# A chunk-selecting attention with a gated convolution: convolution tiles of 64 by 32, score blocks of one bank pair, stores issued by ScalarE

## The chip, the cores and the metric

The kernel runs on one core of a Trainium2 chip. A core has five engines with an instruction stream each: TensorE (PE, with weight loads shown apart as PEld), VectorE (DVE), ScalarE (ACT), GpSimd (POOL) and SyncE (SP, which here only issues transfers). Sixteen DMA engines move the data. TensorE writes to PSUM, eight banks of 128 partitions by 512 fp32 columns, and the other engines empty them. The metric is the device time of one execution in microseconds; less is better.

## The reference, cut to what matters

Attention over 4 batches of 8 heads, 768 positions of 64 values. Each query takes the six chunks of 32 keys with the highest bound on their scores. The output of all heads, 512 channels, then passes a causal convolution of five taps for each channel, a sigmoid gate and two products with 512 by 512 weights.

```python
ub = sum(maximum(q * k_min, q * k_max))          # for each query and chunk of 32 keys
top_chunks = argsort(where(causal, ub, -1e9))[..., -6:]
mask = sel(top_chunks) & (pos[:, None] >= pos[None, :])
attn = softmax(where(mask, scale * q @ k.T, -1e9))
x = (attn @ v).transpose(0, 2, 1, 3).reshape(B, S, H * D)
for k in range(5):
    gate_pre += conv_w[k] * xp[:, k:k + S, :]     # xp: x with four zero rows ahead
out = (sigmoid(gate_pre) * (x @ w_val)) @ w_out
```

## The kernel before, in words

The work is cut into 16 pairs of heads (`p`), four for each batch. The two heads of a pair lie in the two halves of the 128 partitions (`HP`). For a pair: keys and queries are loaded and transposed on PE (`tr`, line 534), copied out by ACT (540, 576) and reduced by chunk on DVE (546); POOL makes the operands of the chunk bounds (`ksmall`); PE forms the bounds (652 and 667), DVE takes the best eight and compares with the sixth (`cmp`, 716) into `NS`; PE transposes `NS` (726) and the copy is the mask `MT`. `score` writes transposed scores into PSUM: queries against keys (748), then the mask times the table `E` (757) into the same bank. ACT takes the exponential (766), POOL clears the upper triangle of the diagonal blocks (774), PE multiplies with the values (`av`, 797), DVE normalizes (806). The result `on` is brought to channels by time, `xT`, by a transposing DMA (827), for the last pair by PE (822).

`BANKS` lays the lower triangle of scores out in six banks for each head. In the kernel before, `DUO` takes two banks at a time: the score products use tiles of 64 rows by 128 columns, two at once, and the mask products use tiles of 32 by 128, four at once, one for each head and bank. For that `cmp` writes the comparison twice, 32 columns apart.

The convolution multiplies shifted copies of `xT` with diagonal matrices. The letter of `CONV` says how, pair by pair:

- Q (pairs 0 to 10, and 15), `convq`, line 883: tiles of 64 by 64, four at once. The weights are split into a high and a low half-precision part, so ten terms. `swap` (849) makes a copy of `xT` with its partition halves exchanged, `XQ`.
- S (pairs 11 to 14), `conv`, line 863: tiles of 128 by 32, four at once, six steps. Its operand `XS` holds 32 channels in four versions (two time shifts, two for high and low weights). It is made by a detour: `xw` (839) writes `xT` to a scratch tensor in DRAM, `xs` (845) reads it back in four transfers.

The diagonal matrices are built on POOL early in the kernel: `WQ` (476) in ten products, `WD` (445) in four. ACT then takes the tanh (889). For each batch, PE forms the values (`val`, 913), DVE gates them (921), PE multiplies with the output weights (937), ACT copies out with a factor of 0.5 (947; in the last batch DVE every second one, 944), and SP stores (952), 24 stores in all.

The order of each engine's stream is computed when the kernel is built. `graph` lists operations with an engine, an estimated length and a sort key from `PERIOD`, `OFF` and `DELTA`; `Graph.schedule` runs a small model of the engines, the banks and the DMA queue, and starts on each free engine the ready operation with the lowest key. Each engine then executes its stream strictly in that order. All the transfers but the two weight loads (`w_big`, on POOL) stand in SP's stream.

Of the kernel before, what the change touches and what calls it, by code (L numbers as in the profile page):

```python
# [19 lines left out]
CH = 32  # L20
# [13 lines left out]
XN = S + 6  # L34

# [15 lines left out]

DUO = ((0, 1), (2, 3), (4, 5))
SCORE = [0.68, 0.70, 0.54]
# [3 lines left out]
for _bi, _segs in enumerate(BANKS):  # L57
    for _col, _jt, _q0, _n in _segs:
        for _i in range(_n // 128):
# [5 lines left out]
PERIOD = 12.9223  # L65
OFF = dict(wdg=199.168, wbig=-116.538, cw=-683.48, load=-91.162, ktr=-51.291, qtr=99.521, kev=-172.346,
           qev=175.061, ksm=-204.505, spl=464.719, vc=678.633, ub=-186.285, top=322.7, selT=-163.727,
           sc=-181.883, ex=-292.07, av=82.464, nrm=333.712, tox=-546.25, xs=-141.243, conv=13.848,
           tanh=-338.872, val=266.063, gv=171.155, out=288.504, ev=-184.148)
# [11 lines left out]
CONV = "QQQQQQQQQQQSSSSQ"  # L81

DELTA = dict(
    wdg=(-1.243, -0.346, -5.29, 3.059, -8.51, 0.295, -11.031, 1.615, 2.466, -0.239, -5.796, 0, -2.239, 11.59,
        -0.038, 0),
    wbig=(0, 0.188, -10.953, -0.19, 0.733, -1.414, -3.353, 1.285, -5.523, -4.485, 38.175, 5.823, 4.557,
        -13.478, 0.421, 0),
    cw=(-18.314, -8.891, -8.843, -0.026, -0.2, 7.762, 12.344, 5.613, 0.06, -2.242, -4.873, -3.047, -3.366,
        0.828, -9.749, -0.011),
    load=(0.214, -1.353, 0.394, -9.477, -20.991, -15.326, -0.566, -8.721, 0.066, -10.887, 23.08, 13.879, 6.207,  # L90
        -4.098, -7.797, -2.716),
    ktr=(3.721, -2.57, -4.059, 0.646, -13.55, 0, 0.055, -1.62, -0.373, 0.436, -1.532, 6.05, 2.065, 1.379, 2.36,
        0.267),
    qtr=(-5.316, -3.862, 0.606, 2.517, 0.494, 0.207, -0.25, -17.411, 1.198, 7.239, -4.482, 0.617, -1.715,
        -0.705, 1.938, 2.43),
    kev=(0, -2.085, -0.198, 0.772, 0.854, 1.732, -0.381, -2.561, 0.048, 6.873, -0.748, -3.931, -1.54, -5.598,
        0, 0),
    qev=(-0.006, -7.153, 2.8, -8.078, -1.913, -4.426, -6.52, -0.93, -1.584, 0.557, 6.224, 0.433, 0, 0.167,
        0.325, 1.843),
    ksm=(-0.516, 1.719, 1.719, 0, -8.166, 5.024, -7.553, -5.823, 0, -13.821, -3.788, 0, 0, 0, 6.169, -3.771),  # L100
    spl=(0, 0, 0.913, -1.823, 3.174, 0.698, 2.737, 0, -0.344, -1.736, -3.55, 8.03, 12.699, 0.056, 12.489, 1.296),
    vc=(-5.408, 8.102, -1.641, -3.236, -11.492, -2.331, -9.437, 2.42, -16.561, 6.032, 0, -2.029, 9.507, 2.124,
        11.374, 1.314),
    ub=(0, 5.87, -1.717, -6.846, -10.954, -7.75, -4.319, 18.215, 2.367, -3.332, -1.487, -3.834, 2.838, -3.08,
        -3.376, 6.316),
    top=(0.011, -14.157, -0.748, -6.694, 0, 1.128, -0.085, 25.804, -19.326, 6.323, 7.216, 7.115, 6.031, 0,
        17.873, -1.714),
    selT=(0.159, 4.322, -11.032, -3.664, 2.206, 2.91, 4.105, -0.067, 0, 2.718, -8.959, -6.512, 0.16, 8.002,
        -0.12, -1.732),
    sc=(2.402, 2.062, 3.966, 0.001, -31.282, -1.168, -3.404, 9.113, -1.06, 0.639, 4.728, -3.231, -1.122,  # L110
        -0.658, -0.515, 0.885),
    ex=(-2.337, 0.461, 5.963, 6.189, 0.222, 2.13, 5.144, 9.503, 6.939, 0.624, 0.959, -13.542, -6.471, -4.563,
        6.731, -4.322),
    av=(0.086, -0.585, 2.526, 2.997, -2.315, -1.993, -1.22, 0, 3.593, 0, 0.163, -0.487, -7.862, -6.595, 1.978,
        -0.201),
    nrm=(-6.208, 0.692, -9.254, 2.271, -0.558, 4.28, 2.998, -3.761, 1.41, 1.599, -8.131, 15.962, -6.789,
        -7.511, -3.999, -3.399),
    tox=(-0.124, 4.074, 0.356, 0.146, 0, -8.203, -3.783, -8.724, -14.631, -6.792, 4.598, -8.206, -0.922,
        -1.434, -0.461, 1.278),
    xs=(-2.03, -2.537, 6.003, -3.321, -6.852, 156.074, 8.152, -17.228, -0.596, 0.102, -1.967, -1.865, -3.351,  # L120
        -1.967, -6.798, 4.494),
    conv=(-1.279, -0.745, -0.991, 1.197, -2.443, 4.986, 5.472, 4.646, -0.942, 1.84, 7.166, -0.096, 2.503,
        -1.052, 4.405, 6.594),
    tanh=(2.324, 0.747, -0.277, -2.803, 0, -3.819, -9.599, -8.531, -3.417, -0.893, -3.327, -0.726, -11.212,
        -0.762, 0.19, -5.493),
    val=(9.122, 0, -6.241, -3.696, 12.326, 2.893, 6.691, -2.508, -1.856, -2.108, -6.259, 37.115, 3.96, 9.385,
        10.567, 13.154),
    gv=(0.221, -7.002, -6.129, -3.775, -3.838, 1.864, 0, 7.518, 5.786, 5.443, -1.952, 0.455, 3.175, 0.33,
        -10.961, 5.879),
    out=(1.189, 1.43, -6.802, 3.456, 1.001, 0.92, -7.795, 60.654, -9.234, 0.84, 0.994, -0.377, 1.598, -2.455,  # L130
        -0.186, 1.785),
    ev=(-3.564, -1.25, -5.306, -0.157, 0, -6.542, 10.476, 4.737, 0.526, 6.5, 7.77, 0.056, 0, 0.402, 3.529,
        -0.709),
)
# [185 lines left out]
def graph(off, period, nbuf):  # L320
# [649 lines left out]
    for o in later:  # L970
        o.deps.add(byname["ksm1"])
# [170 lines left out]
```

## Time and profile before

| | |
|---|---|
| three runs, us | 195.68, 196.44, 196.68 (median 196.44) |
| the profiled execution, us | 197.75 |
| its span, first to last instruction, us | 196.0 |
| TensorE clock granted | 1.0 throughout |
| moved by DMA | 36.01 MB, mean 184 GB/s |
| read from and written to HBM | 24.16 MB and 7.08 MB |

The times are of whole executions; the trace covers the span of the one profiled. Busy time is counted for each engine apart, and a busy TensorE is not one at its peak, since matmuls are pipelined. A group of instructions is given with its line, engine, operation, tiles and number, then its total busy time in us and the mean length of one in ns, then the idle time of the engine ahead of it and what ended that. The chain is followed back from the last instruction, at each step to what released it.

### The profile page before, as it was taken

How to read it: one execution, taken by the hardware profiler on the slowest of the kernel's cores; microseconds unless marked ns; L12 is line 12 of the kernel's file. 1: busy time of each engine (PE TensorE's matmuls, PEld its weight loads, DVE VectorE, ACT ScalarE, POOL GpSimd, SP SyncE). 2: the span in 40 equal slices, each digit the busy share in tenths (PEclk: the TensorE clock that was granted, in tenths of full speed). 3: DMA queues.
4: the chain of work that ended last, by engine and by line, in shares of the span. 5: the costliest groups of instructions: out<-in, count | busy, mean ns of one | idle time of the engine just before them, and what ended most of it. 6: DMA issues, size and time to landing. Idle time of an engine off the chain costs nothing.

```text
span 196.0 us, 7461 instructions
## 1 busy us (share of the span) xinstructions
PE 184.8 (94%) x2926; PEld 118.4 (60%) x2926; DVE 148.3 (76%) x476; ACT 146.7 (75%) x326; POOL 90.4 (46%) x189
## 2 busy tenths in 40 slices
PE   7989898979999999999999999999999997899992
PEld 3666666656757675686675677577656462555540
DVE  6897588979999988879998558998899614062451
ACT  4458999989778879895969897677988977633421
POOL 5589999888445344547262137414363212100000
PEclk9999999999999999999999999999999999999999
DMA  5999999989989998969796998230218839777225
GB/s 134 269 269 207 163 211 205 255 161 225 236 147 222 151 279 190 262 142 222 198 257 181 251 221 162 58 70 2 47 48 251 117 92 282 221 261 251 106 110 211
DMA packets 94917, 36.01 MB, mean 184 GB/s; under 512 B 88226, under 2 KB 91298, under 8 KB 94882
## 3 DMA queue, kind: packets, MB, share of 16 engines
q1 hardware_dynamic: 93826, 34.48, 74.5%
q0 software_dynamic: 1056, 1.05, 3.8%
q8 instruction: 23, 0.38, 0.8%
q14 instruction: 12, 0.10, 0.2%
HBM read 24.16 MB, written 7.08 MB: 159 GB/s over the span
## 4 chain that ended last, share of the span: by engine, by line
PE 74%; DVE 12%; DMA 5%; ACT 4%; SPq 2%; issue 2%; DVEq 0%
PE b L883 10%; PE b L913 10%; PE b L937 9%; PE b L797 9%; PE b L748 8%; PE b L534 8%; PE b L757 5%; PE b L652 5%; DMA xT<-on 3%; DVE km L546 3%; ACT P L766 2%; DMA XS<-scr 2%; PE b L726 2%; PE b L1011 2%; PE b L352 2%; DVE NS L716 2%
## 5 line engine op out<-in xcount | busy, mean ns | idle before, releaser
L766 ACT ACTIVATE P<-b 128x512 f16<-128x512 f32 (+1 forms) x192 | 88.9, 570 | 9.8 <-PE b L757 4.7
L774 POOL TENSOR_SCALAR_AFFINE_SELECT P<-P 128x512 f16<-128x512 f16 (+1 forms) x64 | 33.8, 550 | 60.5 <-ACT P L766 60.4
L546 DVE TENSOR_REDUCE km<-b 128x12 f32<-128x384 f32 x64 | 31.9, 548 | 6.7 <-PE b L534 2.8
L748 PE MATMUL b<-Qh,Kh 64*128 64x128 f16 (+3 forms) x384 | 28.8, 258 | 0.9 <-ACT P L766 0.4
L797 PE MATMUL b<-VA,P 128*128 128x65 f16 x672 | 28.0, 194 | 0.5 <-ACT P L766 0.4
L797 PEld LDWEIGHTS <-P 128*128 128x128 f16 x672 | 24.8, 98 | 4.1 <-issue 1.8
L921 DVE SCALAR_TENSOR_TENSOR gv<-g,b 128x384 f16<-128x384 f32 x32 | 17.5, 550 | 10.2 <-PE b L913 9.1
L913 PE MATMUL b<-xT,wval 128*128 128x384 f16 x128 | 23.8, 326 | 0.0
L937 PE MATMUL b<-wout,gv 128*128 128x512 f16 x96 | 23.5, 379 | 0.0
L947 ACT ACTIVATE osb<-b 128x512 f32<-128x512 f32 x21 | 12.8, 623 | 13.8 <-PE b L937 11.7
L889 ACT ACTIVATE g<-b 128x384 f32<-128x384 f32 x32 | 14.4, 495 | 10.2 <-PE b L883 7.6
L883 PE MATMUL b<-xT,WQ 64*64 64x384 f16 x240 | 21.8, 325 | 0.0
L883 PE MATMUL b<-XQ,WQ 64*64 64x384 f16 x240 | 21.8, 325 | 0.0
L540 ACT ACTIVATE Kh<-b 128x384 f16<-128x384 f32 x32 | 16.2, 520 | 7.0 <-PE b L534 5.2
L748 PEld LDWEIGHTS <-Kh 64*128 64x128 f16 x384 | 12.0, 94 | 12.8 <-issue 11.3
L806 DVE TENSOR_TENSOR on<-b,rcp 128x384 f16<-128x384 f32 x32 | 17.8, 557 | 1.1
L576 ACT ACTIVATE Qh<-b 128x384 f16<-128x384 f32 x32 | 15.7, 531 | 2.7 <-PE b L534 2.7
L757 PE MATMUL b<-MT,E 32*128 32x128 f16 (+4 forms) x352 | 17.6, 259 | 0.0
L883 PEld LDWEIGHTS <-WQ 64*64 64x64 f16 x480 | 12.8, 106 | 6.8 <-issue 2.0
L913 PEld LDWEIGHTS <-wval 128*128 128x128 f16 x128 | 11.5, 98 | 7.9 <-issue 1.3
L622 DVE SCALAR_TENSOR_TENSOR rl<-Qh,ql 128x640 f16<-128x640 f16 x16 | 15.9, 994 | 0.2
L534 PE MATMUL b<-ident,kn 128*128 128x128 f32 x96 | 15.1, 282 | 0.1
(102 smaller groups left out, 320.8 us busy)
## 6 DMA issues: line engine op xcount, KB each, us to landing
kn<-in_k_dram SPq DMA_DIRECT2D x32, 192.0 KB, 3.7
qn<-in_q_dram SPq DMA_DIRECT2D x32, 192.0 KB, 3.7
vn<-in_v_dram SPq DMA_DIRECT2D x16, 384.0 KB, 5.1
out_dram<-osb SPq DMA_DIRECT2D x24, 256.0 KB, 3.1
XS<-scr SPq DMA_DIRECT2D x16, 193.3 KB, 3.3
XQ<-xT SPq DMA_DIRECT2D x24, 96.8 KB, 2.5
scr<-xT SPq DMA_DIRECT2D x4, 193.5 KB
wval<-in_moe_w_val_dram POOLq DMA_DIRECT2D x1, 512.0 KB, 8.6
```

The source lines that it names most:

```text
L534: t.nc.tensor.matmul(out=b[:, j * 128:(j + 1) * 128], lhsT=vv(name, p)[:, 3 * w + j, :], rhs=t.ident, is_transpose=True, start=(j == 0), s ...
L546: t.nc.vector.tensor_reduce(out=vv("km", p)[:, i, w * 12:(w + 1) * 12], in_=bank(("kn", p, w))[:, 0:HB].rearrange("p (c t) -> p c t", t=CH ...
L748: t.nc.tensor.matmul(out=bank(("s", p, bi, hh))[:, col:col + n], lhsT=kh[HP[hh], jt * 128:(jt + 1) * 128], rhs=qh[HP[hh], q0:q0 + n], star ...
L757: t.nc.tensor.matmul(out=bank(("s", p, bi, hh))[:, col + m0 - q0:col + n], lhsT=t.E[rows, jt * 128:(jt + 1) * 128], rhs=mt[rows, m0 - 128: ...
L766: t.nc.scalar.activation(out=t.P[p % 2][hh][bi], in_=bank(("s", p, bi, hh))[:, 0:n], func=AF.Exp, scale=0.125 / QS)
L774: t.nc.gpsimd.affine_select(out=ap, in_=ap, pattern=[[0, n], [1, 128]], compare_op=ALU.is_ge, fill=0.0, base=0, channel_multiplier=-1)
L797: t.nc.tensor.matmul(out=b[:, qt, :], lhsT=t.P[p % 2][hh][bi][:, col:col + 128], rhs=vv("VA", p)[:, hh, jt, :], start=(jt == 0), stop=(jt ...
L806: t.nc.vector.tensor_tensor(out=vv("on", p)[:, :, hh * 64:(hh + 1) * 64], in0=b[:, :, 0:D], in1=rc.unsqueeze(2).to_broadcast([128, NT, D]) ...
L883: t.nc.tensor.matmul(out=bank(("cv", p, r))[HP[c], 0:HB], lhsT=t.WQ[HP[r], k // KSZ, k % KSZ, (p % 4) * 2 + c, :], rhs=x[HP[r], a:a + HB], ...
L913: t.nc.tensor.matmul(out=k[:, 0:HB], lhsT=t.wval[:, ct, et * 128:(et + 1) * 128], rhs=t.xT[:, (4 * b_ + ct) % 8, XL + w * HB:XL + (w + 1) ...
L921: t.nc.vector.scalar_tensor_tensor(out=vv("gv", 4 * b_ + et)[:, sl], in0=vv("g", 4 * b_ + et)[:, sl], scalar=1.0, in1=bank(("val", b_, et, ...
L937: t.nc.tensor.matmul(out=k, lhsT=vv("gv", 4 * b_ + et)[:, s * 128:(s + 1) * 128], rhs=t.wout[:, et, :], start=(et == 0), stop=(et == NCT - 1))
```

## The change

The change replaces four things and computes the order anew.

1. `CONV` becomes R for pairs 0 to 14 and stays Q for pair 15. R uses tiles of 64 rows by 32 columns. The 64 rows are 32 channels twice, for the high and the low part of the weights; the two halves of the partitions hold the two halves of time. Five taps, four groups of channels and two halves of time make 40 matmuls. The diagonal matrices are five products of 128 by 512 on POOL; for the Q of the last pair there are two of 128 by 640.
2. The detour writes `xT` as it lies, 128 partitions outermost, and reads back four transfers of 32 partitions by four runs of 388 elements.
3. `score` takes one bank of each head at a time, and both its products use tiles of 64 by 128. `cmp` writes once.
4. The output stores are issued by ACT, except every second one of the last batch, which stays on SP. The two weight loads become two operations that wait for later pairs.

`PERIOD`, `OFF`, `DELTA` and some of the estimated lengths have new values.

```diff
-DUO = ((0, 1), (2, 3), (4, 5))
-SCORE = [0.68, 0.70, 0.54]
+SCORE = [0.40, 0.435, 0.442, 0.445, 0.35, 0.325]
-CONV = "QQQQQQQQQQQSSSSQ"
+CONV = "RRRRRRRRRRRRRRRQ"
...
-        for j in range(4):
-            G.op(f"wdiag{j}", "POOL", 0.8, 12.3 + 0.1 * j, w_diag(j), r=[("wsel",)], w=[("WD",)])
+        for j in range(KSZ):
+            later.append(G.op(f"wdiag{j}", "POOL", 1.0, key("wdg", 2, 0.5 * j), w_diag(j), r=[("wsel",)], w=[("WD",)]))
...
         for m in range(2):
-            for k in range(KSZ):
-                later.append(G.op(f"qdiag{m}{k}", "POOL", 1.0, key("wdg", 2, 0.5 * (m * KSZ + k)), q_diag(m, k), r=[("qw",)],
-                                  w=[("WQ",)]))
+            last.append(G.op(f"qdiag{m}", "POOL", 1.3, key("wdg", 6, m), q_diag(m), r=[("qw",)], w=[("WQ",)]))
...
-            for r in range(2):
-                t.nc.vector.tensor_tensor(
-                    out=vv("NS", p).rearrange("p i (s c) -> p i s c", s=2)[:, :, :, CH * r:CH * r + NCH],
-                    in0=src,
-                    in1=vv("top", p)[:, :, :, 5:6].to_broadcast([128, NIT, 2, NCH]), op=ALU.is_lt)
+            t.nc.vector.tensor_tensor(
+                out=vv("NS", p).rearrange("p i (s c) -> p i s c", s=2)[:, :, :, 0:NCH],
+                in0=src,
+                in1=vv("top", p)[:, :, :, 5:6].to_broadcast([128, NIT, 2, NCH]), op=ALU.is_lt)
...
+        def score(bi, p=p):
+            def emit():
+                nc, kh, qh, mt = t.nc, vv("Kh", p), vv("Qh", p), vv("MT", p)
+                bb = [bank(("s", p, bi, hh)) for hh in range(2)]
+                segs = BANKS[bi]
+                for si, (col, jt, q0, n) in enumerate(segs):
+                    last = si == len(segs) - 1
+                    m0 = max(q0, SM)
+                    masked = m0 < q0 + n
+                    for hh in range(2):
+                        nc.tensor.matmul(out=bb[hh][:, col:col + n], lhsT=kh[HP[hh], jt * 128:(jt + 1) * 128],
+                                         rhs=qh[HP[hh], q0:q0 + n], start=(si == 0), stop=(last and not masked),
+                                         skip_group_check=True)
+                    if masked:
+                        for hh in range(2):
+                            nc.tensor.matmul(out=bb[hh][:, col + m0 - q0:col + n],
+                                             lhsT=t.E[HP[hh], jt * 128:(jt + 1) * 128],
+                                             rhs=mt[HP[hh], m0 - 128:q0 + n - 128], start=False, stop=last,
+                                             skip_group_check=True)
+            return emit
...
-            t.nc.sync.dma_start(out=t.scr[p % 4].rearrange("c (g n) -> g c n", g=4), in_=t.xT[:, p % 8, XL - 4:XL + S + 2])
+            t.nc.sync.dma_start(out=t.scr[p % 4], in_=t.xT[:, p % 8, XL - 4:XL + S])
+
+        def xs(r, p=p):
+            def emit():
+                for blk in range(2):
+                    t.nc.sync.dma_start(out=vv("XS", p)[HP[r]][blk::2].rearrange("c (g n) -> c g n", g=4),
+                                        in_=t.scr[p % 4].rearrange("(g c) n -> c g n", g=4)[:, :, HB * r:HB * r + XH])
+            return emit
...
+        def conv(p=p):
+
+            x = vv("XS", p)
+            for k in range(KSZ):
+                for g in range(4):
+                    for r in range(2):
+                        t.nc.tensor.matmul(out=bank(("cv", p, r))[32 * g:32 * g + 32, 0:HB],
+                                           lhsT=t.WD[HP[r], k * 16 + (p % 4) * 4 + g, :],
+                                           rhs=x[HP[r], g * XH + k:g * XH + k + HB], start=(k == 0), stop=(k == KSZ - 1))
...
-                t.nc.sync.dma_start(out=t.out[b_, s * 128:(s + 1) * 128, :], in_=vv("osb", 6 * b_ + s))
+                e = t.nc.sync if b_ == B - 1 and s % 2 else t.nc.scalar
+                e.dma_start(out=t.out[b_, s * 128:(s + 1) * 128, :], in_=vv("osb", 6 * b_ + s))
```

## The prediction

> **What bounds the kernel now.** I read the page's engine shares and chain, then the busy time in stretches of 10 us, then the order of time on TensorE, on the queue of SP and on the chain.
>
> ```profile
> PE 184.8 (94%) x2926; PEld 118.4 (60%) x2926; DVE 148.3 (76%) x476; ACT 146.7 (75%) x326; POOL 90.4 (46%) x189
> ...
> PE 74%; DVE 12%; DMA 5%; ACT 4%; SPq 2%; issue 2%; DVEq 0%
> ```
> ```profile
> 20.00:30.00 10.00, 9.10 (x180) 6.49 (x180) 7.75 (x37) 9.82 (x25) 9.51 (x17) 1.00 1.07 193
> ...
> 60.00:70.00 10.00, 10.00 (x189) 6.86 (x189) 9.63 (x38) 8.32 (x20) 4.49 (x11) 1.00 0.98 193
> ...
> 160.00:170.00 10.00, 7.96 (x129) 4.39 (x129) 2.34 (x6) 6.89 (x16) 1.31 (x3) 1.00 0.85 238
> ```
>
> The columns of a stretch are length, busy PE, PEld, DVE, ACT, POOL, clock, DMA share, GB/s. Three stages show. Up to about 50 us ACT and POOL are full (9.82 and 9.51 of 10) and the chain runs over DVE, ACT and short PE pieces: a ramp, not bound by PE. From 50 to 192 us PE is full, except for one hole of 2.04 us at 165.4. There a microsecond of PE is a microsecond of time, as long as the others follow: from 50 to 150 us the stretches add to 88.6 us of DVE and 82.6 of ACT. The last 4 us are copy and store.
>
> What PE spends is read in order of time (start, length, line):
>
> ```profile
> 62.63 0.82 PE L913 MATMUL b<-xT,wval 128*128 128x384 f16 x4
> 63.39 0.35 PE L883 MATMUL b<-xT,WQ 64*64 64x384 f16 x2
> ...
> 65.14 0.60 PE L748 MATMUL b<-Qh,Kh 64*128 64x512 f16 x4
> 65.68 0.39 PE L757 MATMUL b<-MT,E 32*128 32x512 f16 x4
> 66.01 0.82 PE L913 MATMUL b<-xT,wval 128*128 128x384 f16 x4
> ...
> 171.76 1.17 PE L863 MATMUL b<-XS,WD 128*32 128x384 f16 x24
> 172.85 1.04 PE L937 MATMUL b<-wout,gv 128*128 128x512 f16 x4
> ```
>
> From start to next start: a Q convolution takes 1.75 us (63.39 to 65.14), an S convolution 1.09 (171.76 to 172.85), a score block of two banks 0.87, in two parts of 0.54 and 0.33. At the rate of a 384-column step, 0.16 us (the four value matmuls above, 0.65 us in an unbroken row), Q is 10 steps and S is 6: 1.60 and 0.96. Each carries about 0.13 more. The two parts of the score block are 1024 and 512 columns, 0.427 and 0.213 at the same 2.4 columns per ns, so each part carries 0.115 more. So each change of tile shape costs about 0.12 us.
>
> **What the Trainium skill says.** "TensorEngine Tiling (Array Packing)", Tiling Modes, lists 64×32 as eight independent tiles and says that changing the tiling mode drains TensorE. The trace agrees with the drain, 0.12 us; it has no 64×32 tile. "TensorE: Matmul & The Clock Gate", LDWEIGHTS, gives a load as columns over 1.2 ns: an estimate of 27 ns for 32 columns. Here 40 loads of 64 columns fit into a Q convolution's 1.75 us, less than 40 times 53 ns, so loads of different tiles overlap. "DMA: Bandwidth & Descriptors" says of the engines of a DMA (Why a DMA increments its semaphore by 16 and not by 1) that their number is the largest up to 16 dividing both slowest dimensions: 4 for the old scratch write (four groups outermost), 16 for the new. Its landing is not shown, so this is not confirmed. The same page (Issuing engines are not separate DMA queues) says that another issuer saves only sequencer time.
>
> **The change part by part.**
>
> Convolution. R has five taps, with the high and low weights in the two halves of 64 rows, and eight tiles at once: 5 steps of 0.16 plus 0.14, 0.94 us. Not shown in this trace; lower bound 0.92, upper 1.20 if all 40 loads of 27 ns stood in line (1.07) plus the drain. I take 0.94, because S holds full rate with four streams. Q to R saves 0.81 us in eleven pairs, of which the first convolution stands at 47 us in the ramp: 10 x 0.81 = 8.1 after 50 us. S to R saves 0.15 x 4 = 0.6. Together 8.7.
>
> Scores. The pairing of two banks on 32-row tiles goes; each bank is a block of its own, scores and mask both on 64-row tiles. Before: score columns 2688 and mask columns of the longer of two 448 + 512 + 384, in all 4032 / 2.4 = 1.68 us, plus 9 shape changes x 0.115 (entry, middle and exit of three blocks) = 2.71 per pair. After: 2688 + 2432 mask columns = 2.13 us, plus two changes for each group of adjacent blocks. Three groups give 2.82, six 3.51. I take between four and five groups, 3.17, because a block needs two free banks and ACT frees two in 1.2 us (two exponentials of 0.617), while PE has other work in between. That is +0.46 per pair (bounds +0.11 and +0.80); about twelve pairs score after 50 us: +5.5 (1.3 to 9.6). Net PE after 50 us: -3.2, from -7.4 to +0.9. With ACT and DVE as full as above in a fixed order I count 70%: **-2.2**.
>
> DVE and POOL.
>
> ```profile
> L716 DVE TENSOR_TENSOR NS<-mub,top 128x240 f16<-128x240 f32 x24 | 10.0, 457 | 0.1
> ...
> L476 POOL TENSOR_TENSOR WQ<-id,qw 128x512 f16<-128x512 f32 x10 | 10.9, 1110 | 0.0
> ```
>
> The comparison of L716 is made once instead of twice per pair: 0.46 us of DVE a pair, 0.40 in the first four. The weights on POOL were ten products of 1.11 and four of 0.83 (L445), 14.4 us of the first 50; they become five of 1.11, with two more for the last pair that wait for pair 4's key products. In the ramp this could take away four comparisons on the chain, 1.6 us; but ACT is full there and would be late next, so I take **-0.8** (0 to -1.8). After 50 us DVE is not the bound, and its saving is only the room that lets PE's saving through. The later weight loads (POOL, two issues of 0.75 to 0.94 us) stay ahead of the first value matmuls: nothing, while the first value block still comes after 60 us.
>
> Queue of SP, DMA and the end.
>
> ```profile
> 62.14 1.16 SPq L849 DMA_DIRECT2D XQ<-xT  x2
> ...
> 147.63 2.43 SPq L845 DMA_DIRECT2D XS<-scr  x4
> 150.11 0.59 SPq L839 DMA_DIRECT2D scr<-xT  x1
> 150.75 0.46 SPq L952 DMA_DIRECT2D out_dram<-osb  x1
> ```
> ```profile
> 153.39 5.69 DMA xT<-on
> 159.10 0.57 SPq L839
> 162.84 4.32 DMA XS<-scr
> ```
>
> A swap costs SP 1.16 us, a detour 0.59 + 2.43 = 3.02: +1.86 in eleven pairs. Twenty-one of 24 stores leave SP, at 0.34 each (the median of L952): -7.1. In bytes a detour becomes 193 KB written and 388 read, 581 where a swap moved 194 and the old detour 967: 387 x 11 - 386 x 4 = +2.7 MB on 36.0. SP's loads run without a rest to 117 us; about eight pairs' detours fall before that, +15 us less six stores. The lead that pays for it: pair 15's first key load is issued at 110.7 and its key transposes come at 140.8. I cost the slip at nothing while this lead covers it.
>
> At the end the chain is the last batch's detour: transpose 5.69, write, reads, 4.32 to land, and then PE had stood idle 2.04 us. The new detour has as many DMAs, but no store stands between them on SP, and PE reaches it with less behind it. I take **-0.7** (-2.0 to +4.0).
>
> Stores on ACT. Each is one issue in ACT's stream, behind its own copy (L947, 0.62 us). Lower bound 0, if ACT's sequencer runs ahead; upper 0.34 plus a wait of some 0.2 for the copy, 11 us in 21 stores. Behind a waiting store stand the exponentials, and for these AV on PE. ACT is 17% idle there; I take **+1.0** on the end, up to +5.
>
> Sum: -2.2 - 0.8 - 0.7 + 1.0 = -2.7. The profiled execution took 197.75 us (span 196.0 and 1.75 around it), so 195.05 against it; the runs' median of 196.44 is 1.3 lower, and from it **193.7 us**.
>
> **The rivals.**
> 1. Forecast, 191.5 to 195.4: chance 0.37 (0.35 faster, 0.02 same).
> 2. The convolution's gain is eaten by shape changes: six separate blocks, +9.6 against -8.7, so +0.9 - 0.8 - 0.7 + 1.0 = +0.4, 196.8. For it: nearly every score block of the profile has other work behind it. Against: free banks come in pairs and the blocks of a pair are ready together. Chance 0.20 (0.02 faster, 0.10 same, 0.08 slower).
> 3. More gain: three groups, -7.4, of which 80% counts with a lighter DVE (-5.9), ramp and end -1.5, stores +0.4: 189.4. Chance 0.08.
> 4. Slower: SP and DMA become the bound. Loads and detours share SP's one stream; where the slip is longer than the lead, PE waits for keys or for XS. In the middle the lead is only some 7 to 12 us (keys issued at 41.3 and 56.9 are transposed at 48.7 and 68.7), and four or five detours slip it by 1.86 each, 7 to 9. It decides once the slip is longer than that; with queueing (transfers took 2.5 to 5.7 us to land) I price it at 6.8 beyond the forecast: 200.5. For it: DMA busy at 0.98 in that stretch; against: the lead grows to 25 us later, and no PE wait for loads is seen now. Chance 0.26, all slower.
> 5. Stores block ACT: +5 in place of +1, 197.7. Chance 0.09 (0.01 same, 0.08 slower).
>
> That eight tiles don't run together is inside the bound of 1.20: +0.26 x 15 = 3.9 us, which turns the forecast into rival 2 or 5 and is counted there.
>
> **How the numbers follow.** About 0.5% is what a measurement of this kernel can tell from no change. Faster 0.35 + 0.02 + 0.08 = 0.45; same 0.02 + 0.10 + 0.01 = 0.13; slower 0.08 + 0.26 + 0.08 = 0.42. The predicted time is that of the forecast, 193.7. The range of 189.0 to 201.5 leaves out part of rivals 3 and 4.
>
> **What would show it.** Right: 40 convolution matmuls with 0.92 to 0.96 us to the next work; score blocks in four to five groups, 3.1 to 3.3 us a pair with their entries; one L716 row of half the count; PE without holes from 50 us on. Wrong: convolutions at 1.1 or more; PE idle before XS or before key transposes (rival 4); ACT idle in front of exponentials next to a store (rival 5); issues on SP well over 0.6 us after 117 us. A ramp that gains more than 2 us would say that DVE, not ACT, ran it.

## The result, and the profile after

The changed kernel took 203.95 us, the median of four runs (202.17 to 207.75), against 196.56 for the kernel before: a ratio of 1.035, interval 1.028 to 1.043. The forecast was 193.7 with a range up to 201.5. The profiled execution took 203.69 us, with a span of 202.0. Some executions of any kernel here are a few per cent slower than the others; ratios are taken without these, medians with them.

First the shares of the engines and the chain, from the page of the changed kernel.

```profile
PE 180.4 (89%) x2981; PEld 120.1 (59%) x2981; DVE 143.0 (71%) x456; ACT 145.3 (72%) x326; POOL 87.7 (43%) x182
...
PE 55%; DMA 13%; DVE 11%; ACT 11%; SPq 5%; issue 3%; ACTq 0%; DVEq 0%
```

TensorE's work fell as intended, from 184.8 to 180.4 us, and VectorE's from 148.3 to 143.0. Yet the span grew by 6.0 us, so TensorE's idle time went from 11.2 to 21.6. On the chain its share fell from 74% to 55%, and DMA's rose from 5% to 13%: TensorE no longer bounds this kernel without interruption. Where the idle time lies is read from the busy time in stretches (length, then busy PE, PEld, DVE, ACT, POOL, clock, DMA share, GB/s), first of the changed kernel, then of the kernel before.

```profile
60.00:70.00 10.00, 9.73 (x171) 6.84 (x177) 9.49 (x21) 9.04 (x23) 5.28 (x11) 1.00 0.81 170
70.00:80.00 10.00, 7.56 (x165) 4.88 (x142) 6.99 (x25) 4.67 (x12) 2.99 (x9) 1.00 1.12 189
80.00:90.00 10.00, 9.11 (x169) 6.61 (x168) 8.13 (x27) 6.59 (x17) 4.48 (x10) 1.00 1.11 206
90.00:100.00 10.00, 8.59 (x134) 5.10 (x129) 6.34 (x23) 8.16 (x18) 4.16 (x10) 1.00 0.89 211
100.00:110.00 10.00, 6.61 (x116) 4.28 (x116) 5.87 (x14) 5.83 (x15) 2.75 (x7) 1.00 0.95 207
```
```profile
70.00:80.00 10.00, 10.00 (x177) 6.68 (x171) 8.56 (x24) 8.26 (x19) 4.98 (x12) 1.00 1.04 235
80.00:90.00 10.00, 10.00 (x188) 7.23 (x183) 8.89 (x31) 9.40 (x22) 4.87 (x11) 1.00 0.85 187
90.00:100.00 10.00, 10.00 (x160) 6.58 (x159) 9.56 (x29) 8.13 (x18) 4.46 (x10) 1.00 0.85 221
100.00:110.00 10.00, 10.00 (x165) 5.64 (x166) 8.86 (x39) 7.91 (x18) 3.54 (x8) 1.00 0.84 212
```

From 70 to 110 us 8.1 us are lost, in a stage where the kernel before had TensorE at 10.00 in every row. TensorE, VectorE, ScalarE and GpSimd are all less busy there, apart from one row of ScalarE, so none of these took over as the bound; they wait together. Only the share of the DMA engines is higher, 0.89 to 1.12 against 0.84 to 1.04. What TensorE waited for in the changed kernel (who, at which line, for what; total, times, longest, us):

```profile
PE b L524 <- DMA qn<-in_q_dram: 6.9, 4, 3.4
PE b L847 <- DMA XS<-scr: 2.7, 2, 1.5
...
PE b L737 <- ACT Kh L530: 1.3, 1, 1.3
```

It waits for query loads (their transposes are line 524), then for a detour. In the stage from 70 to 110 us the queries make up 6.6 us in three waits, a detour 1.3 and keys 0.2: the 8.1 that were lost. The queue of SP around the longest of these waits (start, length of the issues, line, number):

```profile
82.64 2.01 SPq L512 DMA_DIRECT2D qn<-in_q_dram  x2
84.74 0.49 SPq L509 DMA_DIRECT2D vn<-in_v_dram  x1
85.28 4.17 SPq L512 DMA_DIRECT2D kn<-in_k_dram  x4
89.54 6.12 SPq L827 DMA_DIRECT2D XS<-scr  x8
95.70 0.59 SPq L822 DMA_DIRECT2D scr<-xT  x1
96.39 1.57 SPq L810 DMA_TRANSPOSE xT<-on  x1
98.01 5.35 SPq L512 DMA_DIRECT2D qn<-in_q_dram  x4
```

There is no gap: four query loads stand behind eight detour reads of 6.12 us, a scratch write and a transposing transfer. The chain of the changed kernel goes through just these (start, length, what):

```profile
85.28 1.50 SPq L512
...
88.60 5.17 DMA kn<-in_k_dram
93.91 0.53 PE b L524 x3
...
97.14 0.78 DVE top L696 x10
97.92 0.04 SPq L810
98.01 1.22 SPq L512
99.27 5.77 DMA qn<-in_q_dram
105.18 0.85 PE b L524 x6
```

SP, DMA, PE, DVE, SP, DMA, PE: the end is set by a loop through SP's stream, in which the flight of a load, over 5 us, counts in full. The transposing transfer closes the loop: it stood at SP from 96.39 to 97.96 until VectorE was done, at 97.92, and the query loads behind it stood with it. The median landing of a key or query load was 4.6 and 4.5 us, against 3.7 before.

### The profile page after: what moved, and what is told of

The parts are those of the page before. It is cut to its first block, busy times and chain, and to the rows that moved or that the text cites. A ratio compares the mean times of both kernels' runs of the same rounds, so it can differ in the third digit from the quotient of the medians.

```text
span 202.0 us, 7589 instructions
## 1 busy us (share of the span) xinstructions
PE 180.4 (89%) x2981; PEld 120.1 (59%) x2981; DVE 143.0 (71%) x456; ACT 145.3 (72%) x326; POOL 87.7 (43%) x182
## 4 chain that ended last, share of the span: by engine, by line
PE 55%; DMA 13%; DVE 11%; ACT 11%; SPq 5%; issue 3%; ACTq 0%; DVEq 0%
PE b L921 8%; PE b L780 8%; PE b L897 8%; PE b L737 8%; PE b L524 7%; ACT P L751 6%; DMA qn<-in_q_dram 6%; PE b L742 5%; PE b L847 5%; SPq L512 4%; DVE km L536 3%; PE b L642 3%; DMA kn<-in_k_dram 3%; DMA XS<-scr 2%; DVE rl L612 2%
## 5 line engine op out<-in xcount | busy, mean ns | idle before, releaser
L759 POOL TENSOR_SCALAR_AFFINE_SELECT P<-P 128x512 f16<-128x512 f16 (+1 forms) x64 | 37.6, 607 | 54.0 <-ACT P L751 53.6
L737 PE MATMUL b<-Qh,Kh 64*128 64x128 f16 (+3 forms) x384 | 40.4, 259 | 1.9 <-ACT Kh L530 1.3
L536 DVE TENSOR_REDUCE km<-b 128x12 f32<-128x384 f32 x64 | 32.4, 546 | 13.5 <-PE b L524 9.1
L742 PE MATMUL b<-MT,E 64*128 64x128 f16 (+4 forms) x352 | 37.3, 256 | 0.0
L737 PEld LDWEIGHTS <-Kh 64*128 64x128 f16 x384 | 18.2, 94 | 12.9 <-issue 7.8
L566 ACT ACTIVATE Qh<-b 128x384 f16<-128x384 f32 x32 | 15.0, 510 | 15.0 <-PE b L524 14.9
L742 PEld LDWEIGHTS <-E 64*128 64x128 f16 x352 | 17.4, 95 | 5.2 <-issue 2.4
L524 PE MATMUL b<-ident,qn 128*128 128x128 f32 x96 | 14.0, 278 | 6.9 <-DMA qn<-in_q_dram 6.9
L847 PE MATMUL b<-XS,WD 64*32 64x384 f16 x600 | 16.3, 324 | 3.9 <-DMA XS<-scr 2.7
L612 DVE SCALAR_TENSOR_TENSOR rl<-Qh,ql 128x640 f16<-128x640 f16 x16 | 16.7, 1046 | 1.9 <-ACT ql L589 1.9
L629 POOL CAST VA<-vn 128x768 f16<-128x768 f32 x16 | 13.2, 838 | 9.4 <-PE b L742 6.7
```

The costliest lines, as they stand in the source:

```text
L524: t.nc.tensor.matmul(out=b[:, j * 128:(j + 1) * 128], lhsT=vv(name, p)[:, 3 * w + j, :], rhs=t.ident, is_transpose=True, start=(j == 0), s ...
L536: t.nc.vector.tensor_reduce(out=vv("km", p)[:, i, w * 12:(w + 1) * 12], in_=bank(("kn", p, w))[:, 0:HB].rearrange("p (c t) -> p c t", t=CH ...
L612: t.nc.vector.scalar_tensor_tensor(out=vv("rl", p), in0=vv("Qh", p)[:, 128:S], scalar=0.0, in1=vv("ql", p), op0=ALU.is_gt, op1=ALU.mult)
L737: nc.tensor.matmul(out=bb[hh][:, col:col + n], lhsT=kh[HP[hh], jt * 128:(jt + 1) * 128], rhs=qh[HP[hh], q0:q0 + n], start=(si == 0), stop= ...
L742: nc.tensor.matmul(out=bb[hh][:, col + m0 - q0:col + n], lhsT=t.E[HP[hh], jt * 128:(jt + 1) * 128], rhs=mt[HP[hh], m0 - 128:q0 + n - 128], ...
L759: t.nc.gpsimd.affine_select(out=ap, in_=ap, pattern=[[0, n], [1, 128]], compare_op=ALU.is_ge, fill=0.0, base=0, channel_multiplier=-1)
```

## The experiments

Times are medians. The kernel before, run beside these, took 196.3 to 197.8 us; ratios are to it. Four theories of why SP's transfers are late: A, the bytes; B, SP's time to issue each; C, the loads' place in SP's order; D, the number of transfers in flight. D comes from the program's listing, in which the hardware transfers of SP and ACT take eight completion semaphores in turn (a completion semaphore is raised when a transfer has landed) and each waits for the landing of the one that had its semaphore before (number in the stream, line, transfer, waits; SP's, then one store of ACT's):

```
66 L512 DMACopy kn_137<-in_k_dram 128x6x64 [waits DMAHW5_49,PE_49]
67 L512 DMACopy kn_137<-in_k_dram 128x6x64 [waits DMAHW6_49]
178 L937 DMACopy out_dram<-osb_200 128x512 [waits DMAHW7_49,Activation_49]
```

Whether SP was ever held by such a wait can be read from the times of issues and landings in the traces. In the changed kernel 169 of SP's transfers reuse a semaphore, and each time the transfer before on it had landed 0.8 us or more before SP came to the new one. So this wait held SP nowhere, in the stage from 70 to 110 us either, and D in this form falls for SP's stream. It held two stores of ACT's, for 1.4 us in all.

### Fewer bytes, another issuer, another order

The first three vary the changed kernel. The detour reads of pairs 3 and later fetch one of the four runs, and the convolution computes with what stands in the rest of its buffer:

```diff
+ng = 4 if p < 3 else 1
-    out=XS...rearrange("c (g n) -> c g n", g=4), in_=scr...[:, :, HB * r:HB * r + XH])
+    out=XS...rearrange("c (g n) -> c g n", g=4)[:, 0:ng], in_=scr...[:, 0:ng, HB * r:HB * r + XH])
```

> The changed kernel in its own order; from pair 3 on each of the four reads of a detour fetches one of its four runs (the convolution then works on old data, so the output is not the reference's). SP issues as many transfers, 291 KB less are moved per pair, some 3.5 MB in all. Theory A (the DMA engines' capacity is what delays the key and query loads): the holes of PE between 70 and 110 us, 8 us, mostly close, ratio to the kernel before at or under 1.00. Theory B (SP's time to issue, 0.6 us per transfer, delays them): the holes stay, ratio 1.02 to 1.035. Theory C (the loads stand too late in SP's order): ratio 1.02 to 1.035.

206.45 us, 1.048 (1.043 to 1.054): 3.5 MB less, no gain. TensorE's waits in this kernel:

```profile
PE b L715 <- ACT g L874: 3.9, 1, 3.9
PE b L524 <- DMA qn<-in_q_dram: 3.5, 2, 2.8
```

The wait for queries halved; in its place ACT stood still from 102.9 to 106.9 us, until a query load of SP's that had started at 102.97 and taken 3.86 us was down, and then issued a store. ACT's stores were held so five times in this run, 8.5 us in all. So one stall took the place of another, and A is not refuted: that fewer bytes buy no time was seen only together with these stalls.

The value loads issued by ACT:

```diff
 if name == "vn":
-    t.nc.sync.dma_start(...)
+    t.nc.scalar.dma_start(...)
```

> The changed kernel in its own order, with the sixteen value loads issued by ACT at the same place of the order. The same bytes; SP has 16 issues of 0.5 to 0.6 us less, some 9 us. Theory A: no gain, ratio 1.03 to 1.04. Theory B: the queries of 77, 88 and 105 us come earlier by what SP saved up to there, 3 to 6 us; ratio 1.00 to 1.015. Theory C: about as theory A.

209.29 us, 1.063 (1.057 to 1.069). TensorE still waits 6.7 us for queries. SP's relief bought nothing, though ACT's own stalls are mixed in.

All loads moved up past at most three other operations of SP:

```diff
 order = fill(G, order, t)
+order = earlier(order, 3, ("kn", "qn", "vn"))
```

> The changed kernel; each load of keys, queries or values moved up in SP's stream past at most three transfers of other kinds, never ahead of the release of its buffer; every other engine's stream is the same. The same bytes and issues. Theory C: the loads' waits of PE go, ratio under 1.01. Theories A and B: the total up to there is unchanged, and what is moved behind is the detours; loads gain only what the detours lose, so the holes move from L524 to L847; ratio 1.015 to 1.04.

221.91 us, 1.130 (1.122 to 1.137). The move pushed the load of the convolution weights back; TensorE waited 13.5 us for these alone (line 415), and 8.1 for detours. A cleaner trial is told below.

### What a transfer costs in the kernel before

A detour's transfers, unused, beside each swap of pairs 0 to 10; then the same transfers with 32 bytes a row:

```diff
+if p < 11:
+    t.nc.sync.dma_start(out=t.dscr[p % 2], in_=t.xT[:, p % 8, XL - 4:XL + S])          # e5: 16 columns
+    if p > 0:
+        for r in range(2):
+            for blk in range(2):
+                t.nc.sync.dma_start(out=XS[HP[r]][blk::2], in_=t.dscr[(p - 1) % 2]...)  # e5: 16 columns
```

> The kernel before in its own order and with its own convolutions, and beside each swap of pairs 0 to 10 one scratch write and four reads of the size of the new detour, which nothing uses (the reads take the scratch of the pair before, so SP does not wait). 55 issues and 6.4 MB more. If the traffic of the detour is what slows the changed kernel (theories A and B), this one slows too: ratio 1.02 to 1.06, with PE waiting for keys and queries between 60 and 120 us. If the new order is at fault (theory C) the lead of the loads of the kernel before, 16 us and more, takes it up: ratio 1.00 to 1.01.

> As the run before with added detours, but each of the 55 added transfers moves 32 bytes per row (0.1 MB in all instead of 6.4). The built program gives the hardware transfers of SP and ACT eight completion semaphores in turn, so a transfer is issued only when the one about eight before it has landed. Theory D (the number of transfers in flight is the limit, whatever their size): nearly the whole slowing of 11.6% stays, ratio 1.05 to 1.11. Theory A (capacity of the DMA engines): nothing is left, ratio 1.00 to 1.01. Theory B (SP's time to issue alone, 0.5 to 0.6 us each): 1.03 to 1.06, with the waits ahead of the issues unchanged.

219.92 us, 1.116 (1.109 to 1.123), and 218.37 us, 1.110 (1.104 to 1.116). The trace counts 51 transfers, 11 writes and 40 reads, not the 55 of the expectation (the first pair has no reads). That is 23.4 and 21.9 us for 51 transfers, 0.46 and 0.43 us each, though the first move 6.2 MB and the second 0.1. In this kernel, where SP had seemed to have room, the number costs, and the bytes next to nothing. No issue of SP's was held by a semaphore in either kernel, so this is not D. It fits B: the small transfers took SP 0.59 us each to issue (median), 30 us in all, of which 21.9 show in the time. From the second kernel, the DMA issues (KB each, median us to land) and what TensorE waited for:

```profile
XS<-dscr SPq DMA_DIRECT2D x40, 1.0 KB, 2.0
```
```profile
PE b L891 <- DMA XQ<-xT: 13.8, 7, 3.2
```

One kilobyte takes 2.0 us to land. The Trainium skill, "DMA: Bandwidth & Descriptors", Anatomy of one DMA, gives a fixed cost of about 2.0 us, beside a part that grows with the size, for transfers issued by GpSimd. These are SP's, and the measured size is the same.

### Half the reads, fewer and larger transfers, the stores

In the changed kernel, from pair 3 on, the read of one of the two copies is left out (its rows keep what stands in the buffer); then a write that puts each row down twice, and two reads in place of four; then all stores on SP:

```diff
-for blk in range(2):
+for blk in range(2 if p < 3 else 1):                                       # e6
...
-in_=t.xT[:, p % 8, XL - 4:XL + S])
+in_=t.xT[:, p % 8, XL - 4:XL + S].unsqueeze(1).to_broadcast([128, 2, S + 4]))   # e7
...
-e = t.nc.sync if b_ == B - 1 and s % 2 else t.nc.scalar
+e = t.nc.sync                                                              # e8
```

> The changed kernel in its own order; from pair 3 on a detour reads back only the rows of one of its two copies (the other rows keep old data, so the convolution is not the reference's): 24 transfers and 2.4 MB less. The run that took 3.5 MB away and left the number of transfers did not gain. Theory D: 24 transfers at the 0.43 us that each cost in the kernel before, some 8 to 10 us where the loads wait; the holes of PE between 70 and 110 us close; ratio 0.985 to 1.01. Theory A: no gain, 1.03 to 1.05.

> The changed kernel in its own order with a detour of three transfers in place of five: the write puts each row down twice (386 KB), and each of two reads fetches 64 partitions. The result is the same, 30 transfers less, 3 MB more. Theory D: faster than the changed kernel by 6 to 10 us, ratio 0.98 to 1.01. Theory A: slower than it, ratio 1.04 or more.

> The changed kernel in its own order with all stores issued by SP again. The number of transfers is the same; ACT no longer stands behind the landing of a transfer of SP (2.2 us at 141 us). If stores on ACT cost what the prediction feared, the ratio falls to 1.00 to 1.02; if they are a small matter, it stays at 1.025 to 1.045.

Half the reads: 197.0 us, 0.998 (0.995 to 1.001), 7 us less. Double write: 206.75, 1.039 (1.029 to 1.048), no gain from 30 transfers fewer with 3 MB more; ACT's stores were held for 6.6 us in this run. Stores on SP: 205.73, 1.048 (1.043 to 1.053); so putting the stores back on SP wins nothing.

### Value loads by POOL

POOL's queue is neither SP's nor on the eight semaphores. In the changed kernel, in the one before as a control, with the scratch writes on POOL too, and with all stores on SP:

```diff
-    t.nc.sync.dma_start(out=dst, in_=...)                  # value loads; e11: scr writes too
+    t.nc.gpsimd.dma_start(out=dst, in_=...)
```

> The changed kernel with the 16 value loads issued by POOL instead of SP: same bytes, same order, but 16 transfers fewer in SP's stream and among the eight completion semaphores that SP's and ACT's transfers share. A (bytes), C (order): no gain, 203 to 205 us. B (SP's time) and D (number in flight): 16 x 0.40 us (the cost of one added small transfer, 21.9 us in 55) = 6.4 us less, about 197.5, and TensorE's waits for query loads (6.9 us in the changed kernel) fall below 3. POOL pays some 0.9 us for each issue, which it has to spare (43% busy).

> The control: the same move of the 16 value loads to POOL in the kernel before, where TensorE waits for no load. All theories: within 1% of 196.5 us; a gain of the size of the last run's (6 us) would say that the move helps for a reason that has nothing to do with the detours.

> The changed kernel with the value loads and the 15 scratch writes issued by POOL: 31 transfers fewer on SP and its semaphores, same bytes. B and D: up to 12 us less than the changed kernel, bounded by TensorE's 180.4 us of work plus some 11 us of idle time as in the kernel before, so 191 to 194. A and C: 203 to 205. Against it: each scratch write then waits in POOL's order, in front of the causal masks and the key products, so a detour may come later by 1 to 3 us.

> The changed kernel with the value loads on POOL and all 24 stores on SP: ACT issues no transfer and can't be held by one of SP's. SP then carries 21 stores more and 16 loads fewer. B (SP's own time): 21 x 0.34 - 16 x 0.6 = -2.5 us against the changed kernel, about 201, and 4 above the run with the value loads alone moved. D (the eight in flight, shared by both engines): the stores count alike on either engine, so the same as the run with the value loads alone moved, less what ACT's waits cost there (0 to 2).

209.37 us, 1.066 (1.057 to 1.075); the control 200.48, 1.020 (1.015 to 1.026); with the writes 207.24, 1.055 (1.045 to 1.064); with the stores 209.78, too scattered (204.34 to 210.30) to place. POOL spent 17.0 us on 16 issues, 1.06 each, and the control shows that the move costs 4 us by itself. Taken off, e9 stands at some 205 (an estimate, if the costs add up), still no better than the changed kernel: the forecast of 197.5 from B and D missed. TensorE still waited 4.8 us for queries in e9, but ACT's stores were held for 7.7 us there, so the run doesn't measure SP's time by itself, and B isn't refuted by it. Nor does anything here speak for the issuer as a remedy; the Trainium skill ("DMA: Bandwidth & Descriptors", Issuing engines are not separate DMA queues) says that another issuer saves only the sequencer's time, and here that saving doesn't show.

### No reads, three transfers, and order alone

The scratch laid out by halves, two writes and one read of 128 partitions with rows of 3.1 KB (e13); no read from pair 3 on (e14); the loads of pairs 6 to 15 moved up past three operations (e15); e13 with e15 (e16):

```diff
+for r in range(2):                                                         # e13
+    t.nc.sync.dma_start(out=scr[r].rearrange("c g n -> g c n"), in_=t.xT[:, p % 8, XL - 4 + HB * r:XL - 4 + HB * r + XH])
+t.nc.sync.dma_start(out=vv("XS", p), in_=scr.rearrange("r c g n -> (r c) (g n)").unsqueeze(1).to_broadcast([64, 2, 4 * XH]))
...
+for blk in range(2 if p < 3 else 0):                                       # e14
...
+loads = [o for o in order if o.name[:2] in names and int(o.name[2:]) >= 6] # e15
```

> The changed kernel with a detour of three transfers instead of five: the scratch memory is laid out half by half, so two writes (one for each half of the sequence) and a single read of all 128 partitions with rows of 3.1 KB, broadcast to the two copies; the same bytes within 1%, the same result, 30 transfers fewer on SP, 384 packets fewer per detour. D and B (number of transfers): 30 x 0.29 (the gain of the half detour, 6.95 us over 24) to 0.40 us = 8.7 to 12 less, so 192 to 195.5. A (bytes): 203 to 205. C (order, latency of each step behind the next): no gain, or slower if the single read lands later than the four short ones (3.5 us).

> The changed kernel with no detour read from pair 3 on (48 transfers and 4.7 MB less; the convolution of these pairs computes with what stands in its buffer, the scratch is still written): what the kernel would take if its detours cost nothing. If the prediction's sum is right apart from the detours' traffic: 193.7 or lower, down to 190. If it stays over 200, neither bytes nor number of the detours is the cause, and the order of the loads (C) or the scores on TensorE are.

> The changed kernel with the loads of pairs 6 to 15 alone moved up past at most three other operations of SP (the run that moved all loads also pushed the load of the convolution weights back, which cost 13.5 us by itself). C: the waits of TensorE for query loads (6.9 us) go, 196 to 198. B and D: what the loads gain the detours' reads lose; TensorE's waits move from qn to XS, 203 to 207.

> Both together: detours of three transfers, and the loads of pairs 6 to 15 moved up past three operations of SP. If the number of transfers is the cause, as in the run with three transfers alone (192 to 196), since nothing waits any more; if the order adds its own share, 2 to 4 us less than that run.

Without reads: 194.32 us, 0.984 (0.978 to 0.989). Three transfers: 211.34, 1.068 (1.061 to 1.075). Order alone: 213.83, 1.071 (1.063 to 1.079). Both: 215.17, 1.087 (1.079 to 1.094). Only the first gained.

The three transfers differ in more than their number. Their writes put the four groups of channels outermost, as the old detour did, where the changed kernel's write has the 128 partitions outermost. In the traces a write of this kind raises its semaphore in 5 steps, one about 1.0 us after the issue and four at the end, and lands after 5.6 us (e13, 97 KB). That of the changed kernel takes 16 steps and 3.5 us (193 KB), the old one in the kernel before 5 steps and 5.4 us (all medians). That agrees with the 4 and 16 DMA engines that the prediction counted and couldn't confirm, and it means that e13 and e16 made the writes slower along with cutting the number. ACT's stores were also held, for 9.5 and 10.0 us.

TensorE's long stretches (columns as above) in the kernel before, the changed one, and the one without reads:

```profile
50.00:110.00 60.00, 59.89 (x1062) 40.35 (x1063) 55.43 (x187) 49.51 (x112) 25.84 (x58) 1.00 0.92 208
```
```profile
50.00:110.00 60.00, 51.60 (x946) 35.13 (x944) 44.95 (x143) 44.15 (x102) 26.59 (x57) 1.00 0.99 201
```
```profile
50.00:110.00 60.00, 57.35 (x1081) 39.38 (x1075) 50.45 (x171) 49.49 (x114) 27.66 (x59) 0.99 0.95 194
```

With the reads out, TensorE wins back 5.75 of the 8.3 us it had lost here. 1.3 of them are the wait for a detour itself, which this kernel no longer has. On SP's queue of the kernel without reads, the query loads for which TensorE had waited longest go out at 92.68 instead of 98.01:

```profile
82.96 5.79 SPq L512 DMA_DIRECT2D kn<-in_k_dram  x4
88.79 0.60 SPq L822 DMA_DIRECT2D scr<-xT  x1
91.35 1.23 SPq L810 DMA_TRANSPOSE xT<-on  x1
92.68 2.43 SPq L512 DMA_DIRECT2D qn<-in_q_dram  x4
```

When order alone is changed, what the loads gain the detours lose: TensorE's waits move from queries to `XS`, 13.3 us in six waits. So C falls in this form: moving the loads up doesn't help.

### Three transfers without ACT's stalls

In the kernel with three transfers TensorE's longest waits were for ACT next to stores (`osb` 3.2, tanh 2.0 us). The last two runs move the stores of the first three batches to POOL, with five transfers and with three:

```diff
-e = t.nc.sync if b_ == B - 1 and s % 2 else t.nc.scalar
+e = t.nc.gpsimd if b_ < B - 1 else (t.nc.sync if s % 2 else t.nc.scalar)
```

> The changed kernel with the stores of the first three batches issued by POOL, whose queue is neither SP's nor one of the eight semaphores: ACT can no longer stand behind one of SP's transfers, and SP gets nothing in return. If the coupling of ACT's stores with SP's transfers is a main cause: TensorE's waits for ACT next to a store go, and the time falls to 198 to 200. If the detours' transfers are the cause by themselves: within 1% of the changed kernel, 202 to 206; TensorE still waits for query loads and XS. POOL pays 18 issues of about 1.06 us (what a value load cost it), which by itself can cost as much as the 4 us of the control.

> The same with the detour of three transfers. In the run with three transfers and stores on ACT, TensorE's longest waits were for ACT (osb 3.2, tanh 2.0, keys 1.7 us), next to stores. If the number of transfers is the cause and those ACT waits hid its gain: 6 to 10 us below the last run, 192 to 197, and below the kernel before. If fewer but larger transfers only land later (no gain from the number): no better than the last run, 202 to 208.

204.59 us, 1.038 (1.026 to 1.051), and 204.90, 1.042 (1.033 to 1.051). No store of ACT's was held in either. Freeing ACT bought nothing that can be seen, though POOL's 18 issues may hide some 4 us, as in the control; and three transfers in place of five, again with the slower writes, are no better. SP's queue of the last kernel:

```profile
84.57 2.55 SPq L512 DMA_DIRECT2D qn<-in_q_dram  x2
87.22 1.07 SPq L509 DMA_DIRECT2D vn<-in_v_dram  x1
88.34 4.24 SPq L512 DMA_DIRECT2D kn<-in_k_dram  x4
92.68 1.46 SPq L829 DMA_DIRECT2D XS<-scr  x2
94.19 1.18 SPq L823 DMA_DIRECT2D scr<-xT  x2
95.47 1.65 SPq L810 DMA_TRANSPOSE xT<-on  x1
97.17 4.17 SPq L512 DMA_DIRECT2D qn<-in_q_dram  x4
```

The reads now take 1.46 us in place of 6.12, yet the query loads go out at 97.17, hardly before 98.01: the whole stream had already come to this place some 3 us later. From the scratch write ahead of the first of these key loads (52.46 and 51.95 us) to the loads of pair 12 (103.40 and 101.38), the changed kernel issues 54 transfers in 50.9 us and the last one 45 in 49.4, so 0.94 us and 1.10 us each. Fewer and larger transfers leave the stream as long as it was. Part of the time that the reads give back goes into standing at the transposing transfers, which wait for VectorE: the same five of them take SP 10.5 us in the last kernel and 6.7 in the changed one. The two in the middle, changed kernel and last:

```profile
69.41 2.59 SPq L810 DMA_TRANSPOSE xT<-on  x2
```
```profile
68.29 4.45 SPq L810 DMA_TRANSPOSE xT<-on  x2
```

No kernel that computes all of the result beat the kernel before.

## Why the prediction was wrong

**The step that failed** is the one on SP's queue: "I cost the slip at nothing while this lead covers it." The lead of 30 us was read from the order of the kernel before, for keys, in which pair 15's keys are issued at 110.7. What the runs showed in its place is a wait of 8.1 us between 70 and 110 us, 6.6 of it for queries, of which the prediction counted no lead, and only 0.2 for keys. The changed kernel has its own order. On SP's queue pair 9's keys are issued at 74.9 instead of 59.4, pair 11's at 87.7 instead of 75.9, and pair 10's queries at 98.0 instead of 72.6. A slip is not yet a wait: pair 13's keys go out at 122.8 instead of 87.9, yet from 110 to 140 us TensorE is never idle, because their use has moved as well. A lead belongs to an order; where the order is computed anew it can't be carried over as cover.

**Rival 4** named what happened, with its place (the middle) and its sign: TensorE waits for loads and for `XS`, though for queries more than for the keys that it names. Its price, 6.8 us beyond the forecast, was too low: the time is 10.3 beyond it (203.95 less 193.7). Its slip of 7 to 9 us, five detours by 1.86, left out that the loads' order changes as well. That the cause is the detour reads is shown by the two runs that leave reads out: 7.0 us less for half of them, 9.6 for all from pair 3. Leaving them out takes away both the transfers and the convolutions' own wait for them, so these runs don't tell the two apart, except that the query loads went out 5.3 us earlier. No run that changed the stores, the issuer or the order of the loads won anything back, though the runs with POOL pay for its issues.

Which property of the reads counts isn't settled. The semaphores (D) never held SP in the changed kernel. Bytes were cut without the number, and the number without the bytes, and neither gained; both fell together in the two runs that did. But each of the runs without gain changed something else too: ACT's stores were held for 8.5 us in e1, e7 moves 3 MB more, and e13, e16 and e18 have slower writes. SP's own time (B) has the best support, from the kernel before, where 51 small transfers cost 21.9 us; that it rules in the changed kernel too is not shown.

A part of the lateness belongs to the new order itself. In the kernel without reads pair 9's keys go out at 75.9 and pair 11's at 87.4, as late as in the changed kernel, and TensorE still waits 4.2 us for keys and queries; only from there on do the two draw apart, pair 12's 95.2 against 103.4, pair 15's 132.9 against 143.5.

**The terms of the sum.** The convolution is as forecast: 0.94 us, in the chain of the changed kernel

```profile
114.56 0.94 PE b L847 x40
```

so eight tiles run together at full rate. The scores come out at the forecast too, but partly by luck. In one pair they stand in three groups, of which this is the second, of three banks, 1.55 us to the next work,

```profile
65.56 0.39 PE L737 MATMUL b<-Qh,Kh 64*128 64x512 f16 x2
...
66.89 0.21 PE L742 MATMUL b<-MT,E 64*128 64x128 f16 x1
67.11 0.55 PE L524 MATMUL b<-ident,kn 128*128 128x128 f32 x3
```

and 0.93 and 0.33 for the others; with three entries of 0.115 that is 3.16 us. The forecast took 3.17 for four to five groups, and 2.82 for three: fewer groups than it thought, and each dearer. The whole kernel has 48 groups in 16 pairs, three for each on average. Rival 2 with its six groups falls; rival 3 had their number right and not its gain. In all TensorE's work after 50 us fell by 4.3 us (from 140.1 to 135.8), where -3.2 was forecast. The comparison on DVE is made half as often, and DVE fell by 5.3 us. The ramp gained nothing: in the first 50 us TensorE was busy 44.6 us, before 44.7, so -0.8 should have been 0 (the clock granted was 0.83 from 20 to 30 us of this execution, so a small gain may be hidden). At the end, TensorE's idle time from 160 to 180 us is 2.55 against 2.04 before, so -0.7 should have been about +0.5. The stores on ACT were taken at +1.0; against all stores on SP they are nothing or a gain up to 1.8 us (203.95 and 205.73, with intervals that touch), so rival 5 falls as an account of the loss. Its sign is there once, at its size in the forecast: TensorE waited 1.3 us at 144 behind a held store (last section).

The part of the sum on TensorE's work was about right, then; the sum failed in what it took as hidden. With nearly all detour reads left out the kernel takes 0.984 of the time before, 3.2 us less out of 196.6, where -2.7 was forecast. That these two agree so well is again partly luck: the run also has no idle time from 160 to 180 us, since its last convolutions wait for no read, and the terms for the ramp and the end were off by 0.8 and 1.2.

## What to carry to other kernels

A transfer that nobody waits for is free only in the order in which that was read. Where a change adds transfers to the one stream that also brings the operands, take the slip from the loads that come next behind them (all kinds, not keys alone), in the new order and in the stage where the lead is shortest, and price what exceeds the lead as wait. Before one builds such a change, an execution of it with the extra transfers left out tells what it can be worth at most; here that was 3.2 us for a detour that costs three times as much.

## What the runs showed of the hardware

- A transfer added to SP's queue cost the kernel before 0.43 us at 1 to 4 KB and 0.46 us at about 100 to 200 KB. Reads of 1 KB land in 2.0 us, a detour read of 24 KB (e1) in 2.6, one of 97 KB in 3.5 (medians).
- A write to DRAM with four groups outermost landed in 5.4 us (193 KB, kernel before) and 5.6 us (97 KB, e13), raising its semaphore in one early step and four late ones; one of 193 KB with 128 partitions outermost landed in 3.5 us, in 16 steps.
- A store issued by ACT can wait for a transfer of SP's, through the semaphores that both use in turn in these programs. In the changed kernel the queue of ACT shows it (start, length, line, and in brackets the idle time ahead); `osb` was done at 141.4, and the scratch write that had the store's semaphore before, started at 140.30, landed at 143.58:

```profile
140.78 0.60 ACT L931 ACTIVATE osb<-b 128x512 f32<-128x512 f32 x1 [0.24 <-ACT Kh L530]
141.27 0.87 ACT L566 ACTIVATE Qh<-b 128x384 f16<-128x384 f32 x2
143.65 0.34 ACTq L937 DMA_DIRECT2D out_dram<-osb  x1
144.04 0.49 ACT L530 ACTIVATE Kh<-b 128x384 f16<-128x384 f32 x1 [1.91 <-DVE rcp L788]
```

- An issue on POOL occupied it for 1.06 us; moving 16 value loads there cost the kernel before 4 us.
- Tiles of 64 by 32, eight at once, ran 40 matmuls of 384 columns in 0.94 us, the full rate that four tiles of 128 by 32 had shown.
